# Gated attention and channel MLP on one core: both heads' maxima fetched by one transfer, first stacks loaded two units sooner, two PSUM pairs renamed in turn

## The chip, the cores and the metric

The kernel runs on one core of one Trainium2 chip. A time is the device time of one execution in microseconds (us); the profile is one execution recorded by the hardware, and its span runs from the first to the last recorded instruction. Engines are called as the profile calls them: PE (matmuls), DVE, ACT, POOL, and SP, which here only issues transfers. ACT issues some transfers too.

## The reference

```python
def _A_ref(x, wqkv, wo):
    B, S, D = x.shape
    H = 32; Dh = D // H; W = 256
    qkv = (lambda x, *d: x.transpose(*d))((x @ wqkv).reshape(B, S, 3, H, Dh), 2, 0, 3, 1, 4)
    q, k, v = qkv[0], qkv[1], qkv[2]
    scores = jnp.einsum("bhqd,bhkd->bhqk", q, k) * (Dh ** -0.5)
    idx = jnp.arange(S)
    mask = (idx[:, None] - idx[None, :] >= 0) & (idx[:, None] - idx[None, :] < W)
    scores = jnp.where(mask[None, None], scores, -1e9)
    p = _softmax(scores, axis=-1)
    o = jnp.einsum("bhqk,bhkd->bhqd", p, v)
    return (lambda x, *d: x.transpose(*d))(o, 0, 2, 1, 3).reshape(B, S, D) @ wo
...
def _B_ref(x, w1, b1, w2, b2):
    y = _layernorm(x, axis=-1)
    h = _gelu(jnp.einsum("bsd,df->bsf", y, w1) + b1)
    return jnp.einsum("bsf,fd->bsd", h, w2) + b2
...
g = _sigmoid((x * gate_w).sum(-1, keepdims=True))
a = _A_ref(x, A_wqkv, A_wo)
b = _B_ref(x, B_w1, B_b1, B_w2, B_b2)
return g * a + (1 - g) * b
```

There are 2048 tokens (S) of 512 numbers, 32 heads of 16 numbers with a window of 256 tokens, and a hidden width of 1792. All is float32.

## The kernel before

Products are made in several passes: a number is split into a high part, rounded to a shorter format, and a low part, the remainder, and high x high, low x high and high x low are added up. The work has three stages.

**First stage: projections.** A list of `units` is run one by one. A unit is one product of 12 matmuls of 512 columns: `qk_unit(g, t, c)` for a group g of 8 heads, q or k (t), and a chunk c of 512 tokens, or `v_unit(b)` for 128 tokens. `plan` says what is done before which unit: `at(n, fn)` puts fn before unit n, and what was put first under one n is done first. `after(k, fn)` postpones fn by k units. The result of a `qk_unit` is split and written to a DRAM tensor `qkd[g, t]`, which holds for each of the 8 heads a stack of rows: high, low and high again for k (high, high, low for q), 48 rows in all, and 2 gap rows. `gaps(g)` fills the gap rows from rows of the SBUF tensor `qk` that were set to a constant. `load_stacks(p, a, n)` brings for the four heads of step p (two pairs `pr` of heads, of two heads `e` each) n columns from column a back into `qk`, 14 partitions down, so that the two heads of a pair lie above each other. The result goes to `qs` (q) and `ks` (k), which are halves of `qk`. Besides, weights (`load_w`, the line L228), rows of x for the layer norm's sums (`stat_unit`, L468), and constants (`load_consts`) are loaded. From unit 16 on the first scores are made as well.

**Second stage: attention, mixed with the MLP's first half.** A string `ORDER` lists the steps: S is `s_pair`, the scores of 128 queries for two heads, of which only the row maximum is wanted; T is `st_pair`, the scores again, transposed, from which the maximum is subtracted within the matmul (that takes two more rows: high and low part of the maximum on the side of q, -1 on the side of k), with the exponential and the mask after it; P is `pv`, the product with v; f is one matmul pair of the MLP. After four blocks of queries `put_max` carries their maxima to the rows of `qs`: `parts` splits them on POOL, `turn` transposes them on DVE, `put` writes them to a DRAM tensor `md` (from ACT's queue in this stage), and `rest` loads them from `md` (SP's queue). They come 6, 13, 21 and 28 steps later (`CHAIN`). An S, T or f step takes its two PSUM banks from `ring`: `choose()` takes out a name at a place that `PICK` gives, and the name goes back at the end.

**Third stage:** the second half of the MLP, the output projection and the gate.

SP carries its transfers out in the order of the program, and each is issued when what it needs has come; a wait holds up all transfers behind it. The program gives every transfer one of 8 semaphores in turn, so that at most 8 of both queues are under way.

Of the kernel before, what the change touches and what calls it, by code (L numbers as in the profile page):

```python
# [13 lines left out]
F32R = mybir.dt.float32r  # L14
# [8 lines left out]
DH = 16  # L23
# [8 lines left out]
HG = H // NG  # L32
VW = 17
VR = 560
EPS = 1e-5
NEG = -3.0e38
U8 = mybir.dt.uint8
# [24 lines left out]
def gated_mix_kernel(ctx, tc: tile.TileContext, xt, x2, wq0, wqk, wv, wo, xa, gw, w1, w2, b1, b2, out):  # L62
# [96 lines left out]
    osc = dram.tile([8, 128, S], F32, name="osc")  # L159
    stat = dram.tile([2, 2, S // 2], F32, name="stat")  # L160
    hp = dram.tile([NCH, FT, 128, C], F32, name="hp")
    qkd = {(g, t): dram.tile([HG, 50, S], F32R, name=f"qk{g}_{t}") for g in range(NG) for t in range(2)}

    open_pool("w")
    open_pool("ring")
# [52 lines left out]

    def gaps(g):
        for t in range(2):  # L220
            sp.dma_start(f32(view(qkd[g, t], [50 * S, HG], [S, 2], [1, S], off=48 * S)), f32(ks[0][112:128]))

    wq, wvs, xh, xl = {}, [], [], []

# [87 lines left out]
    def qk_out(g, t, c, o):  # L312
        d = qkd[g, t]
        h, l = t2(F32R), t2(F32R)
        copy(h, o)
        lo_part(l, o, h)

        def put(eng, k, s):
            eng.dma_start(f32(view(d, [S, DH], [50 * S, HG], [1, C], off=k * DH * S + c * C)), f32(s))

        if g:
            put(act, 0, h)
        late = (2, 1, 1, 1)[c] if not g else 1
        after(late, lambda: [put(sp, k, h) for k in ((0, 1 + t) if not g else ())])
        after(late, lambda: put(sp, 2 - t, l))

    def double(g, c, t):
        fr, to = (f32(view(qkd[g, t], [S, DH], [50 * S, HG], [1, C], off=k * DH * S + c * C)) for k in (0, 1 + t))
        sp.dma_start(to, fr)

    def v_unit(b):
# [12 lines left out]
    def load_stacks(p, a, n):  # L344
        g, j = divmod(p, 2)
        held_cols[p] = a + n
        for t in (1, 0):
            src = view(qkd[g, t], [S, 98], [100 * S, 2], [1, n], off=4 * j * 50 * S + a)
            sp.dma_start(f32(qk[14:112, 2 * t:2 * t + 2, a:a + n]), f32(src))

    mxs, done = {}, set()

    def s_pair(p, qb, pr):
        if qb == 0 and pr == 0:
            mxs[p] = small("mx", 2, (128, 2, 2, NB))
        assert qb * 128 < held_cols[p]
        n = min(qb + 1, 3) * 128
        t0 = qb * 128 + 128 - n
        o = two()
        for e in range(2):  # L360
            r, k = ((0, 62), (64, 112))[e]
            pe.matmul(o[:, e, :n], qs[pr][r:k, qb * 128:qb * 128 + 128], ks[pr][r:k, t0:t0 + n],  # L362
                      start=True, stop=True)
        m = mxs[p][:, pr, :, qb]
        if qb < 2:
            for e in range(2):
                sc = small("scr", 2, (128, 256), BF16)
                dve.tensor_tensor_reduce(out=sc[:, :n], in0=o[:, e, :n], in1=wide[:, 256 - n:], scale=1.0, scalar=NEG,
                                         op0=ALU.add, op1=ALU.max, accum_out=m[:, e:e + 1])
        else:  # L370
            dve.copy_predicated(o[:, :, :128], tri, o[:, :, 256:384])  # L371
            dve.tensor_reduce(m, o[:, :, :256], mybir.AxisListType.X, ALU.max)  # L372
        if pr and qb % 4 == 3:
            put_max(p, qb - 3)

    def put_max(p, a):
        mx = mxs[p][:, :, :, a:a + 4]
        sm = {}
        md = dram.tile([2, 2, 2, 4, 128], F32R, name=nm("md"))

        def parts():
            m = sm["m"] = small("nm", 2, (128, 2, 2, 2, 4), F32R)
            pool.tensor_copy(m[:, 0], mx)
            lo_part(m[:, 1], mx, m[:, 0], pool)

        def turn():
            sm["s"] = small("ms", 2, (128, 32))
            dve.transpose(sm["s"], f32(sm["m"]).rearrange("p a b c d -> p (a b c d)"))

        def put(eng=None):  # L390
            (eng or (act if spot[0] > 99 else sp)).dma_start(f32(view(md, [32, 4], [128, 32], [1, 32])), sm["s"])

        def rest():
            done.add(("m", p, a // 4))
            for k in range(2):
                src = view(md, [512, 2], [1024, 2], [1, 512], off=2048 * k)
                sp.dma_start(f32(qk[62 + k:113 + k:50, :2, a * 128:a * 128 + 512]), f32(src))
# [574 lines left out]
```

## Time and profile before

| | |
|---|---|
| runs | 691.52, 687.71, 690.15 us; median 690.15 |
| profiled execution | 688.9 us, of which the span takes 686.9 |
| mean granted PE clock | 0.999 |
| busy share of the span | PE 99%, DVE 69%, ACT 56%, POOL 39% |
| transfers | 137.91 MB, mean 201 GB/s |

The first stage lasts until 144 us, the second until 486 us. In a timeline row the first number is the start in us from the span's start, the second the length, then engine (SPq: the issue of a transfer), line, operation, what is written from what, the shapes, the count of merged instructions, and in brackets the engine's idle time before it with what ended that. A row of waits has the total in us, the number of times, and the longest. A row of the chain has start, length and what it was.

### The profile page before, as it was taken

The page shows a single profiled execution, that of the slowest core. Times are in us where ns is not written, and L with a number is a line of the kernel's source. Part 1 is how long each engine was busy: PE and PEld are TensorE (multiplying, and loading weights), DVE is VectorE, ACT ScalarE, POOL GpSimd, SP SyncE. Part 2 cuts the span into 40 slices and gives each one's busy share as a digit, 9 for nine tenths or more (in the row PEclk, how much of TensorE's full clock was granted, in tenths as well). Part 3 has the DMA queues.
Part 4 walks back from the last instruction along what each step waited for, and adds up shares of the span by engine and source line. Part 5 has one row for each costly group of instructions (what it writes and reads, how often), then busy time and mean ns, then how long its engine had stood idle before and what let it go on. Part 6 is the DMA issues. An engine that isn't in the chain of part 4 may idle for free.

```text
span 686.9 us, 15594 instructions
## 1 busy us (share of the span) xinstructions
PE 680.0 (99%) x5674; PEld 532.7 (78%) x5674; DVE 473.3 (69%) x970; ACT 387.4 (56%) x637; POOL 266.6 (39%) x622
## 2 busy tenths in 40 slices
PE   9999999999999999999999999999999999999997
PEld 6887777877767877778787777777787888888886
DVE  6737789958767788787777777856575545556454
ACT  6437554456777776767667777677633224123221
POOL 5800166335566664756655666568000000000000
PEclk9999999999999999999999999999999999999999
DMA  8999898776755867656775655436886440841701
GB/s 314 361 314 280 263 272 254 223 234 201 227 169 180 249 207 228 190 166 220 222 233 189 177 184 164 159 127 211 291 235 209 140 171 5 270 132 45 251 0 62
DMA packets 89620, 137.91 MB, mean 201 GB/s; under 512 B 13160, under 2 KB 36648, under 8 KB 89416
## 3 DMA queue, kind: packets, MB, share of 16 engines
q1 hardware_dynamic: 81384, 128.72, 59.3%
q10 hardware_dynamic: 8160, 8.19, 3.8%
q8 instruction: 45, 0.74, 0.5%
q14 instruction: 31, 0.25, 0.1%
HBM read 81.53 MB, written 54.30 MB: 198 GB/s over the span
## 4 chain that ended last, share of the span: by engine, by line
PE 90%; DMA 6%; DVE 1%; SPq 1%; issue 0%; ACT 0%; DVEq 0%; ACTq 0%
PE ps_b L651 22%; PE ps_a L881 16%; PE ps_b L441 12%; PE ps_d L308 12%; PE ps_b L418 7%; PE ps_d L338 7%; PE ps_b L362 6%; PE ps_o L850 6%; DMA oa<-osc 1%; DMA md<-ms 1%; DMA ra<-rd 1%; DMA su<-osc 1%; PE ps_d L295 1%; PE ps_x L362 1%; DMA hp<-t 1%; PE ps_x L279 1%
## 5 line engine op out<-in xcount | busy, mean ns | idle before, releaser
L651 PE MATMUL ps_b<-x,w 64*128 64x512 f32 x1344 | 208.1, 393 | 0.1
L881 PE MATMUL ps_a<-x,t 128*128 128x512 f32 x648 | 150.7, 390 | 0.2 <-DVE t L711 0.2
L372 DVE TENSOR_REDUCE mx<-ps_b 128x2 f32<-128x512 f32 x208 | 144.2, 693 | 7.2
L881 PEld LDWEIGHTS ps_a<-x,t 128*128 128x128 f32 x648 | 121.3, 188 | 26.8 <-DVE t L133 0.8
L651 PEld LDWEIGHTS ps_b<-x,w 64*128 64x128 f32 x1344 | 125.9, 186 | 11.1 <-issue 0.6
L371 DVE COPY_PREDICATED ps_b<-tri,ps_b 128x256 f32<-128x256 uint8 x208 | 88.4, 425 | 53.9 <-PE ps_b L362 39.9
L422 POOL TENSOR_SCALAR_AFFINE_SELECT pa<-pa 128x256 f32<-128x256 f32 x192 | 74.2, 413 | 63.8 <-ACT pa L420 63.3
L420 ACT ACTIVATE pa<-ps_b 128x768 f32<-128x768 f32 x96 | 76.8, 812 | 25.5 <-PE ps_b L418 17.0
L418 PE MATMUL ps_b<-qk 64*128 64x384 f32 (+4 forms) x512 | 87.6, 339 | 1.2 <-DMA qk<-md 1.1
L308 PE MATMUL ps_d<-x,w 128*128 128x512 f32 x360 | 84.7, 390 | 0.0
L362 PE MATMUL ps_b<-qk 62*128 62x384 f32 (+3 forms) x472 | 82.3, 344 | 0.0
L308 PEld LDWEIGHTS ps_d<-x,w 128*128 128x128 f32 x360 | 67.3, 188 | 14.5 <-issue 0.5
L420 ACT ACTIVATE pb<-ps_b 128x768 f32<-128x768 f32 (+2 forms) x96 | 66.5, 706 | 18.2 <-PE ps_b L418 14.7
L422 POOL TENSOR_SCALAR_AFFINE_SELECT pb<-pb 128x256 f32<-128x256 f32 x160 | 62.5, 414 | 31.4 <-ACT pb L420 29.7
L707 ACT ACTIVATE t<-t,b1s 128x512 f32<-128x512 f32 x56 | 38.5, 716 | 45.6 <-DMA t<-hp 45.0
L422 POOL TENSOR_SCALAR_AFFINE_SELECT x<-x 128x256 f32<-128x256 f32 x128 | 49.4, 413 | 36.0 <-ACT x L420 35.3
L418 PEld LDWEIGHTS ps_b<-qk 50*128 50x128 f32 (+1 forms) x512 | 48.6, 184 | 17.8 <-DVE mx L372 2.5
L420 ACT ACTIVATE x<-ps_b 128x768 f32<-128x768 f32 x64 | 51.0, 812 | 15.8 <-PE ps_b L418 9.4
L362 PEld LDWEIGHTS ps_b<-qk 62*128 62x128 f32 (+1 forms) x472 | 44.8, 184 | 16.7 <-issue 4.5
L338 PE MATMUL ps_d<-wv,x 128*128 128x512 f32 x192 | 46.7, 394 | 0.0
L850 PE MATMUL ps_o<-w,t 128*128 128x512 f32 x192 | 46.1, 389 | 0.0
L441 PE MATMUL ps_b<-pa,v 128*32 128x128 f32 (+2 forms) x704 | 42.9, 345 | 0.2
(96 smaller groups left out, 753.7 us busy)
## 6 DMA issues: line engine op xcount, KB each, us to landing
qk<-qk SPq DMA_DIRECT2D x112, 196.0 KB
t<-hp SPq DMA_DIRECT2D x56, 256.0 KB
hp<-t SPq DMA_DIRECT2D x54, 256.0 KB
qk<-t SPq DMA_DIRECT2D x48, 256.0 KB
osc<-x SPq DMA_DIRECT2D x31, 256.0 KB
t<-in_w SPq DMA_DIRECT2D x28, 256.0 KB
w<-w SPq DMA_DIRECT2D x28, 256.0 KB
qk<-t ACTq DMA_DIRECT2D x24, 256.0 KB
```

The lines of the kernel that those rows point to most:

```text
L308: pe.matmul(o, a[:, dt * 128:(dt + 1) * 128], b[:, dt * C:(dt + 1) * C], start=n == 0, stop=n == 11)
L338: pe.matmul(o, x[:, a:a + 128], wvs[dt][:, k], start=n == 0, stop=n == 11)
L362: pe.matmul(o[:, e, :n], qs[pr][r:k, qb * 128:qb * 128 + 128], ks[pr][r:k, t0:t0 + n], start=True, stop=True)
L371: dve.copy_predicated(o[:, :, :128], tri, o[:, :, 256:384])
L372: dve.tensor_reduce(m, o[:, :, :256], mybir.AxisListType.X, ALU.max)
L418: pe.matmul(o[:, e, :w], ks[pr][r:k, kb * 128:kb * 128 + 128], qs[pr][r:k, kb * 128:kb * 128 + w], start=True, stop=True)
L420: act.activation(pt[:, :, :w], o[:, :, :w], AF.Exp, scale=0.25)
L422: pool.affine_select(out=pt[:, :, a:a + 128], in_=pt[:, :, a:a + 128], pattern=[[0, 2], [sgn, 128]], base=b, channel_multiplier=-sgn, comp ...
L441: pe.matmul(a[32 * h:32 * h + 32, at:at + w], vs[:, kb, v:v + 32], pts[p, kb][:, h, fr:fr + w], start=n == 0, stop=n == len(parts) - 1, sk ...
L651: pe.matmul(o[:, e], w[kt // 4][r:r + 64, k, m:m + 128], y[r:r + 64, a:a + C], start=n == 0, stop=n == 23)
L850: pe.matmul(a, x[:, g], wos[g][:, k], start=n == 0, stop=n == 11)
L881: pe.matmul(accs[c][b], x[:, b * 128:(b + 1) * 128], w, start=f == 0 and n == 0, stop=f == FT - 1 and n == 2)
```

## The change

It has four parts.

1. *One transfer for the maxima.* The stacks in `qkd` get 52 rows per head instead of 50, so that the gap between the two heads of a pair is four rows, and the second head begins on partition 66. `md` and the tile `nm` are laid out by head first, and `rest` loads four neighbouring partitions (62 to 65) by one transfer where it loaded two partitions by each of two. `load_stacks` brings 100 partitions (14 to 113), where it brought 98. The second head's scores in `s_pair` run over 50 partitions, where they ran over 48.
2. *Gap rows.* They are four rows, of which `gaps` now fills only those between the heads of a pair, for q from rows set to 0 and for k from rows set to -1. Each transfer has 8 pieces of 16 KB where it had 16 of 8 KB.
3. *Places in the plan.* `gaps(0)` stands before unit 7 (was 8), the first `load_stacks` before unit 9 (was 11), and both stand ahead of `load_consts` in the code.
4. *Ring.* It starts as b0, b1, b3, b2.

```diff
+HR = 52
...
-    qkd = {(g, t): dram.tile([HG, 50, S], F32R, name=f"qk{g}_{t}") for g in range(NG) for t in range(2)}
+    qkd = {(g, t): dram.tile([HG, HR, S], F32R, name=f"qk{g}_{t}") for g in range(NG) for t in range(2)}
...
     def gaps(g):
         for t in range(2):
-            sp.dma_start(f32(view(qkd[g, t], [50 * S, HG], [S, 2], [1, S], off=48 * S)), f32(ks[0][112:128]))
+            dst = view(qkd[g, t], [2 * HR * S, 4], [2 * S, 2], [1, 2 * S], off=48 * S)
+            sp.dma_start(f32(dst), f32(qk[116 * t:116 * t + 8, 2:].rearrange("k r s -> k (r s)")))
...
-            src = view(qkd[g, t], [S, 98], [100 * S, 2], [1, n], off=4 * j * 50 * S + a)
-            sp.dma_start(f32(qk[14:112, 2 * t:2 * t + 2, a:a + n]), f32(src))
+            src = view(qkd[g, t], [S, 100], [2 * HR * S, 2], [1, n], off=4 * j * HR * S + a)
+            sp.dma_start(f32(qk[14:114, 2 * t:2 * t + 2, a:a + n]), f32(src))
...
-            r, k = ((0, 62), (64, 112))[e]
+            r, k = ((0, 62), (64, 114))[e]
...
-        md = dram.tile([2, 2, 2, 4, 128], F32R, name=nm("md"))
+        md = dram.tile([4, 2, 4, 128], F32R, name=nm("md"))
...
-            pool.tensor_copy(m[:, 0], mx)
-            lo_part(m[:, 1], mx, m[:, 0], pool)
+            mt = mx.rearrange("p r e b -> p e r b")
+            pool.tensor_copy(m[:, :, 0], mt)
+            lo_part(m[:, :, 1], mt, m[:, :, 0], pool)
...
-            for k in range(2):
-                src = view(md, [512, 2], [1024, 2], [1, 512], off=2048 * k)
-                sp.dma_start(f32(qk[62 + k:113 + k:50, :2, a * 128:a * 128 + 512]), f32(src))
+            sp.dma_start(f32(qk[62:66, :2, a * 128:a * 128 + 512]), f32(view(md, [1024, 4], [512, 2], [1, 512])))
...
+    for g in range(NG):
+        at((7, 16, 20, 24)[g], lambda g=g: gaps(g))
+    for c in range(NCH):
+        at((9, 19, 29, 44)[c], lambda c=c: load_stacks(0, c * C, C))
     at(9, load_consts)
-    for g in range(NG):
-        at((8, 16, 20, 24)[g], lambda g=g: gaps(g))
-    for c in range(NCH):
-        at((11, 19, 29, 44)[c], lambda c=c: load_stacks(0, c * C, C))
...
-    ring += ["b0", "b1", "b2", "b3"]
+    ring += ["b0", "b1", "b3", "b2"]
```

From here the order of the built programs. The line numbers of the changed kernel are one or two higher. The numbers in a name tell one buffer or tensor from another. First SP's queue in the first stage, around units 9 to 12 (t: an SBUF tile; qk0_0 and qk0_1: the stacks in DRAM for q and k of group 0; qk_3_79: the SBUF tensor `qk`), before:

```order
L319 DMA qk0_0_65<-t_63_415 16x8x512
L463 DMA gws_9_99<-in_gw 128x512
L464 DMA b1s_83<-in_b1 128x14
L468 DMA t_64_423<-in_xa 128x512
L228 DMA t_66_426<-in_wqk 128x512
L319 DMA qk0_1_66<-t_68_441 16x8x512 x2
L319 DMA qk0_1_66<-t_69_442 16x8x512
L468 DMA t_70_448<-in_xa 128x512
L349 DMA qk_3_79<-qk0_1_66 98x2x512
L349 DMA qk_3_79<-qk0_0_65 98x2x512
L468 DMA t_72_468<-in_xa 128x512
L228 DMA t_74_471<-in_wqk 128x512
```

And the same rows of SP's queue in the changed kernel:

```order
L321 DMA qk0_0_65<-t_63_415 16x8x512
L351 DMA qk_3_79<-qk0_1_66 100x2x512
L351 DMA qk_3_79<-qk0_0_65 100x2x512
L464 DMA gws_9_99<-in_gw 128x512
L465 DMA b1s_83<-in_b1 128x14
L469 DMA t_64_425<-in_xa 128x512
L230 DMA t_66_428<-in_wqk 128x512
L321 DMA qk0_1_66<-t_68_443 16x8x512 x2
L321 DMA qk0_1_66<-t_69_444 16x8x512
L469 DMA t_70_450<-in_xa 128x512
L469 DMA t_72_468<-in_xa 128x512
L230 DMA t_74_471<-in_wqk 128x512
```

The two stack loads (L349, now L351) have moved ahead of eight transfers: the two constants, two loads of x rows, one weight load, and the three writes that stand between the latter. From the last load of x rows shown on, all stands as before. The gap transfers of group 0 (L221, now L223) stand four rows ahead of these pieces, in the same place before and now, since the order in the code makes up for the earlier unit; only their shape is another, 4x2x4096 where it was 8x2x2048.

In the second stage, SP's queue around the sixth load of maxima, before and then in the changed kernel:

```order
L349 DMA qk_3_79<-qk0_1_66 98x2x256
L349 DMA qk_3_79<-qk0_0_65 98x2x256
L397 DMA qk_3_79<-md_288_2053 2x2x512 x2
L541 DMA t_295_2239<-in_w1 128x512
L349 DMA qk_3_79<-qk1_1_68 98x2x256
```

```order
L351 DMA qk_3_79<-qk0_1_66 100x2x256
L351 DMA qk_3_79<-qk0_0_65 100x2x256
L398 DMA qk_3_79<-md_288_2048 4x2x512
L542 DMA t_295_2233<-in_w1 128x512
L351 DMA qk_3_79<-qk1_1_68 100x2x256
```

Nothing moved there but the second of the two loads of maxima, which is gone; so it is at all 32 places.

Last PE at the first steps of the attention, before and then in the changed kernel (ps_b0 to ps_b3 are the PSUM pairs of the ring):

```order
L362 MATMUL ps_b0_260_1529<-qk_3_79 128x384 x2
L418 MATMUL ps_b1_261_1535<-qk_3_79 128x384 x2
L651 MATMUL ps_b2_262_1541<-x8_142_850,w_218_1285 128x512 x2
L362 MATMUL ps_b3_263_1544<-qk_3_79 128x384 x2
L651 MATMUL ps_b2_262_1541<-x8_142_850,w_218_1285 128x512 x6
```

```order
L364 MATMUL ps_b0_260_1527<-qk_3_79 128x384 x2
L419 MATMUL ps_b1_261_1533<-qk_3_79 128x384 x2
L652 MATMUL ps_b3_262_1539<-x8_142_850,w_218_1283 128x512 x2
L364 MATMUL ps_b2_263_1542<-qk_3_79 128x384 x2
L652 MATMUL ps_b3_262_1539<-x8_142_850,w_218_1283 128x512 x6
```

The matmuls stand as before; the names b2 and b3 are exchanged, here and in all later rows. A pool hands out its banks in the order in which its names are first used: in the built program the third pair (b2 before, b3 now) is banks 4 and 5, and the fourth is banks 6 and 7, before and now.

More of the change, by code (lines that the diff above doesn't have):

```diff
@@ L318, in put @@
         def put(eng, k, s):
-            eng.dma_start(f32(view(d, [S, DH], [50 * S, HG], [1, C], off=k * DH * S + c * C)), f32(s))
+            eng.dma_start(f32(view(d, [S, DH], [HR * S, HG], [1, C], off=k * DH * S + c * C)), f32(s))
         if g:
@@ L327, in double @@
     def double(g, c, t):
-        fr, to = (f32(view(qkd[g, t], [S, DH], [50 * S, HG], [1, C], off=k * DH * S + c * C)) for k in (0, 1 + t))
+        fr, to = (f32(view(qkd[g, t], [S, DH], [HR * S, HG], [1, C], off=k * DH * S + c * C)) for k in (0, 1 + t))
         sp.dma_start(to, fr)
```

## The prediction

> **What bounds the kernel now.** I read the page's first part, then PE's waits, then the chain and the timelines around those waits.
>
> ```profile
> span 686.9 us, 15594 instructions
> PE 680.0 (99%) x5674; PEld 532.7 (78%) x5674; DVE 473.3 (69%) x970; ACT 387.4 (56%) x637; POOL 266.6 (39%) x622
> ```
>
> PE works 680.0 of 686.9 us, so an edit that leaves PE's instructions as they are can gain at most the 6.9 us of idle time. This one leaves them: same matmuls, same columns, same order; only the second head's scores are summed over 50 partitions for 48. Which waits are in the 6.9 us?
>
> ```profile
> PE ps_x L279 <- DVE t L275: 1.3, 1, 1.3
> PE ps_b L418 <- DMA qk<-md: 1.1, 2, 0.9
> PE ps_a L881 <- DVE t L711: 0.2, 1, 0.2
> ```
>
> These are all of PE's waits inside the span, 2.6 us (total, times, longest). The rest stands at the ends, where nothing is changed. Only the middle row touches the change: twice `st_pair` waits for maxima. PE's timeline shows where:
>
> ```profile
> 192.62 0.61 PE L418 MATMUL ps_b<-qk 64*128 64x384 f32 x4 [0.90 <-DMA qk<-md]
> ...
> 255.95 0.44 PE L418 MATMUL ps_b<-qk 64*128 64x384 f32 x2 [0.19 <-DMA qk<-md]
> ```
>
> **One transfer for the maxima.** The chain of waits shows what lies ahead of the two matmuls (start, length, what):
>
> ```profile
> 184.85 4.73 DMA md<-ms
> ...
> 189.65 0.66 SPq L397
> ...
> 190.36 2.13 DMA qk<-md
> 192.49 0.14 issue
> 192.62 0.61 PE ps_b L418 x4
> ```
>
> ```profile
> 249.12 3.92 DMA md<-ms
> ...
> 253.06 0.66 SPq L397
> ...
> 253.76 2.06 DMA qk<-md
> 255.82 0.14 issue
> 255.95 0.44 PE ps_b L418 x2
> ```
>
> The write to `md` lands, SP issues the first load (0.66 us), then the second, and the chain runs through the second: it sets out at 190.36, which is 189.65 plus 0.66 plus a pause of 0.05. SP's timeline shows the pair merged:
>
> ```profile
> 189.65 1.34 SPq L397 DMA_DIRECT2D qk<-md  x2
> ```
>
> With one transfer this second issue falls away, so the maxima land earlier by 190.36 - 189.65 = 0.71 us at the first place and by 253.76 - 253.06 = 0.70 at the second. What is unknown is how long a transfer of four partitions and 16 KB takes to land. The bounds: as long as the 8 KB ones (2.06 and 2.13), or as long as the other 16 KB transfer, `md<-ms` (3.92 and 4.73), which writes memory where this one reads it. With the first the gain is 0.71 of 0.90 and all of the 0.19, **0.90 us**; with the second the load lands 1.1 to 1.9 us later than now, which costs that much at each of the two places, 3.0 us, and opens waits at others. I take the first: it is the same direction, the same piece of 2 KB and the same two tensors.
>
> The other 30 loads have no wait on PE today. They too come 0.7 us earlier, and gain nothing. SP is spared 32 issues of 0.66, 21 us; what does it do with them?
>
> ```profile
> SPq L397 <- DMA md<-ms: 66.5, 28, 4.4
> ```
>
> It waits for the maxima's writes anyway, 66.5 us in 28 places (4.4 the longest), and the transfers queued behind a load of maxima are issued 0.7 us sooner. PE waits for none of them (its three rows of waits name no other transfer), so nothing: 0. What limits the gain: after the first place PE arrives at each later matmul 0.71 us sooner, while writes that were already under way do not. Between 0 and 0.90 us can come back as a new wait; I take 0, since the maxima follow from PE's own scores and move with them.
>
> POOL's two operations on `nm` write their 16 columns in another order: two instructions before and after. Their cover is the 13 to 28 steps between the first of `CHAIN` and the last; the count of elements is the same, so 0; at the two waiting places whatever they take more would show in full.
>
> **The stacks' shape.** Each stack load has 100 rows for 98, 2% more bytes. In the second stage the transfers have room:
>
> ```profile
> 140.00:480.00 340.00, 338.50 (x4140) 258.79 (x4140) 256.89 (x578) 248.76 (x380) 209.14 (x551) 1.00 0.64 197
> ```
>
> (The columns: window, sum, busy PE, PEld, DVE, ACT, POOL, granted PE clock, DMA share, GB/s.) At a share of 0.64, 2% are nothing: 0. How far 100 rows instead of 98 spread over the DMA engines, no row shows; that is part of the rival below.
>
> **Gaps and first stacks, sooner.** Here the transfers are the tight resource:
>
> ```profile
> 10.00:30.00 20.00, 20.00 (x90) 16.57 (x89) 18.14 (x25) 11.10 (x20) 18.68 (x17) 1.00 1.05 390
> 30.00:43.00 13.00, 13.00 (x59) 10.78 (x58) 4.92 (x8) 3.52 (x6) 3.02 (x2) 1.00 0.91 293
> 43.00:56.00 13.00, 13.00 (x62) 10.27 (x61) 6.85 (x22) 8.09 (x21) 0.00 (x0) 1.00 0.97 324
> ```
>
> The DMA share is 0.91 to 1.05, yet PE is busy throughout. SP's timeline:
>
> ```profile
> 29.04 1.67 SPq L221 DMA_DIRECT2D qk<-qk  x2
> ...
> 34.20 0.60 SPq L463 DMA_DIRECT2D gws<-in_gw  x1
> ...
> 36.55 0.43 SPq L228 DMA_DIRECT2D t<-in_wqk  x1
> 37.08 1.80 SPq L319 DMA_DIRECT2D qk<-t  x3
> 38.92 0.86 SPq L468 DMA_DIRECT2D t<-in_xa  x1
> 39.88 1.33 SPq L349 DMA_DIRECT2D qk<-qk  x2
> 41.32 0.42 SPq L468 DMA_DIRECT2D t<-in_xa  x1
> 41.78 0.43 SPq L228 DMA_DIRECT2D t<-in_wqk  x1
> ```
>
> In the new order the two stack loads (39.88) go out at 34.20, and the eight transfers from `gws` to the `in_xa` of 38.92 follow 1.33 us later. The gap transfers (29.04) keep their place, and the last of their source rows have been set by 19.9:
>
> ```profile
> 16.09 3.84 POOL L207 MEMSET qk<- 32x2048 f32 x2
> ```
>
> Nothing gains by earlier stacks: their first user has no wait. Who loses? The weight load that was ahead of the stacks and is now behind them:
>
> ```profile
> 41.01 0.43 DVE L194 CAST w<-t 128x512 fp32r<-128x512 f32 x1 [4.56 <-DMA t<-in_wqk]
> 41.47 0.69 DVE L133 TENSOR_TENSOR w<-t,w 128x512 fp32r<-128x512 f32 x1
> 42.29 0.69 DVE L133 TENSOR_TENSOR t<-ps_d,t 128x512 fp32r<-128x512 f32 x1
> ...
> 50.05 0.43 DVE L194 CAST w<-t 128x512 fp32r<-128x512 f32 x1 [2.89 <-PE ps_x L362]
> ...
> 54.88 0.08 DVE L368 DVE_READ_ACCUMULATOR2_ANT mx<- 128x1 f32 x1
> ```
>
> It is issued at 36.55 and cast at 41.01, the moment it lands: 4.46 us. The next, of equal size but behind the stack pair, is issued at 41.78 and cast at 50.05: 8.27 us. So a stack pair costs the transfer behind it up to 8.27 - 4.46 = 3.81 us. The first weight load then is issued near 37.9 and lands between 42.3 (its issue + 4.46) and 46.1 (+ 8.27). What it feeds on PE begins here:
>
> ```profile
> 49.71 0.44 PE L362 MATMUL ps_x<-qk 62*128 62x128 f32 x4
> 50.08 3.00 PE L308 MATMUL ps_d<-x,w 128*128 128x512 f32 x12
> ...
> 55.73 0.50 PE L362 MATMUL ps_x<-qk 62*128 62x256 f32 x4
> ```
>
> The product at 50.08 uses the weights that DVE casts from 41.01 on, and the PSUM bank that DVE's 42.29 row reads, which is queued behind the cast. With the cast at 46.1, cast (0.43), remainder (0.69) and that row (0.69) end by 48.0, 2.1 us before PE gets there: hidden. The load behind, of 41.78, no longer has the pair before it and comes sooner or, the path being full all the way, at the same time: 0, since the same bytes go ahead of it as before.
>
> **The ring** exchanges two names. The order of the banks follows from first use, so PE's matmuls stand on the same banks with the same distances: 0, in both directions.
>
> **Sum.** 688.9 of the profiled execution (its span of 686.9 and 2.0 around it) - 0.71 - 0.19 + 0 = 688.0. That execution lies 1.25 below the median of the three runs (690.15), and all four (687.71, 688.9, 690.15, 691.52) spread by 3.8; I take their middle, (688.9 + 690.15) / 2 = 689.5, and forecast 689.5 - 0.9 = **688.6 us**. A change of less than 0.5%, 3.45 us (686.7 to 693.6), can hardly be told from none in a measurement of this kernel.
>
> **Rival 1: the gain doesn't come.** The single transfer of four partitions and 16 KB lands 0.7 us later than two 8 KB ones did, or the next late write takes the wait over. For it: the writes to `md` take 3.92 to 4.73 us in the chain, the largest share, and they aren't touched. Against: SP's second issue is plainly serial. The time: 689.5.
>
> **Rival 2, slower: the new shapes hold the full DMA path longer, and PE stalls in the first stage.** A gap transfer now has four slowest rows (was eight), a stack load 100 (was 98). No row shows what that does to the landing. If fewer DMA engines carry a transfer, those behind it wait. The place is the weight load that DVE casts at 50.05. From there DVE works without a pause to 54.96 (54.88 + 0.08), the last maximum of the scores at 49.71, and the second scores on PE at 55.73 need their PSUM banks back: a margin of 55.73 - 54.96 = 0.77 us. That is the point that decides: if the load comes more than about 0.8 us later, the rest is a stall of PE. Gaps with half the rows, taken to last twice as long, make the load later by their share of the pair's price: two of 128 KB against two of 392 KB, 3.81 x 256 / 784 = 1.24 us. A stack pair that lasts 1.5 times as long, halfway between nothing and double, adds 1.90. By the gaps alone PE stalls 1.24 - 0.77 = 0.5, by both 1.24 + 1.90 - 0.77 = 2.4, by a doubled pair alone 3.81 - 0.77 = 3.0; with the gain of 0.9 that is 689.1, 691.0 and 691.6. Beyond a delay of 0.77 + 0.90 = 1.7 us the kernel is slower than before. I take 691.0. For it: shares of 0.91 to 1.05, and DVE's waits for weights in the rows. Against it: stack loads of 98 rows run in all of the kernel now without making PE wait.
>
> The Trainium skill has a rule on this, on its page "DMA: Bandwidth & Descriptors", section "Why a DMA increments its semaphore by 16 and not by 1": a transfer uses the largest number of engines up to 16 that divides the slowest dimension of both sides, and the page's own example is 100 partitions on 10 engines. By that rule 98 rows go on 14 engines and 100 on 10 (the factor 1.4), gap transfers go from 8 engines to 4 (the factor two), and the loads of maxima from 2 to 4; as an estimate from that page and the pair's 3.81 us, the load at 50.05 comes 0.4 x 3.81 + 1.24 = 2.8 us later and the time is 688.6 + 2.8 - 0.8 = 690.6. No row here shows the engines of one transfer, so the rule is neither borne out nor refuted yet.
>
> **How the numbers follow.** Gain of 0.9 with the first stage hidden: 0.46, at 688.6. Rival 1: 0.17, at 689.5. Rival 2: 0.33, at 691.0. Something not seen here: 0.04. The low end is the fastest run less the gain, 687.71 - 0.9 - 0.2 for the chance of a bit more = 686.6; the high end is rival 2's 691.6 plus 0.7 for the spread of medians = 692.3. All three cases lie inside 0.5%. Faster by more needs the gain and a fast draw: 0.07. Slower by more needs rival 2 beyond its own top or a slow draw: 0.08. That leaves 0.85.
>
> **What the profile of the changed kernel would show.** Right: PE's row of waits for `qk<-md` falls from 1.1 to about 0.2 us, the first place's wait from 0.90 to 0.2, the chain there holds one SP issue, and the chain's `qk<-md` piece is still about 2.1 us. Wrong by rival 1: that piece is 2.8 us or more, or a wait of like size stands at another load of maxima. Wrong by rival 2: PE's timeline has an idle piece ahead of the scores near 55.7 us, released by DVE, and DVE's casts there wait for `in_wqk` past 51 us; in the second stage PE would wait for `qk<-qk`. The forecast falls if PE's busy time itself moves from 680.0 us.

## The result

The changed kernel is slower: 699.29 us median of 6 runs (694.54 to 702.39), the kernel before 690.84 of 6 (687.71 to 692.72); ratio 1.0133, 95% interval 1.0103 to 1.0164. The forecast was 688.6 us, range 686.6 to 692.3. Of all executions in this document one, of 709.70 us in the run b_md4 below, lies more than 1.5% above the fastest of its kernel; it counts as slow and is left out.

The profiled execution took 702.17 us, one of the two slowest of the six, so its losses are larger than the median's. The page:

```profile
span 700.4 us, 15571 instructions
PE 685.5 (98%) x5674; PEld 538.5 (77%) x5674; DVE 473.8 (68%) x970; ACT 385.4 (55%) x637; POOL 267.8 (38%) x622
```

The span grew by 13.5 us: PE is busy 5.5 us longer with the same 5674 matmuls, and idle 8.0 us longer (14.9 for 6.9). PE's waits (total, times, longest) say where the idle time is:

```profile
PE ps_x L364 <- DVE mx L374: 4.3, 3, 3.6
PE ps_x L364 <- DVE mx L370: 2.4, 1, 2.4
PE ps_b L419 <- DMA qk<-md: 2.3, 2, 2.1
PE ps_x L281 <- DVE t L277: 1.3, 1, 1.3
PE ps_a L882 <- DVE t L712: 0.2, 1, 0.2
```

Two rows are new: the first scores (`ps_x`, L364 was L362) wait 6.7 us for DVE. The row of the maxima has not fallen from 1.1, it has grown to 2.3. The same on PE's timeline:

```profile
58.72 0.83 PE L364 MATMUL ps_x<-qk 62*128 62x256 f32 x4 [2.41 <-DVE mx L370]
...
106.07 0.69 PE L364 MATMUL ps_x<-qk 62*128 62x384 f32 x2 [3.64 <-DVE mx L374]
...
202.64 0.62 PE L419 MATMUL ps_b<-qk 64*128 64x384 f32 x4 [0.28 <-DMA qk<-md]
...
247.83 0.44 PE L419 MATMUL ps_b<-qk 64*128 64x384 f32 x2 [2.05 <-DMA qk<-md]
```

The first is the place of rival 2. What leads to it is on the timelines of SP, ACT and DVE. SP's first, and the row of the one wait it has at these loads:

```profile
37.60 0.75 SPq L351 DMA_DIRECT2D qk<-qk  x2
...
39.99 0.65 SPq L230 DMA_DIRECT2D t<-in_wqk  x1
```

```profile
SPq L351 <- DMA qk<-qk: 1.1, 1, 1.1
```

The stacks go out at 37.60, where the prediction had 34.20: SP waits 1.1 us for the gap transfers, and the issues ahead take longer too. The weight load now behind the stacks is issued at 39.99 and cast at 48.77 (DVE's first row below), where it was issued at 36.55 and cast at 41.01. A write of a projection's result, issued at 40.73 behind them, lands at 49.49 (its last completion event), 8.76 us later. ACT issues such writes too, and its next one has the same one of the eight semaphores: it waits for that landing, and ACT's work behind it waits with it. ACT's row after this wait, before and then in the changed kernel, and a later one there:

```profile
43.77 0.63 ACT L471 ACTIVATE waste<-t 128x512 f32<-128x512 f32 x1 [1.51 <-DMA qk<-t]
```

```profile
50.24 0.63 ACT L472 ACTIVATE waste<-t 128x512 f32<-128x512 f32 x1 [7.69 <-DMA qk<-t]
...
56.33 0.58 ACT L137 ACTIVATE t<-ps_d 128x512 fp32r<-128x512 f32 x1
```

So ACT goes on 6.5 us later than before. From 50.24 to the end of the last of these rows it works, or issues, without a pause, and DVE waits for it twice:

```profile
48.77 0.43 DVE L195 CAST w<-t 128x512 fp32r<-128x512 f32 x1 [9.42 <-DMA t<-in_wqk]
...
52.33 0.69 DVE L134 TENSOR_TENSOR t<-ps_d,t 128x512 fp32r<-128x512 f32 x1 [1.80 <-ACT t L137]
...
53.54 0.42 DVE L195 CAST w<-t 128x512 fp32r<-128x512 f32 x1
...
56.94 0.69 DVE L134 TENSOR_TENSOR t<-ps_d,t 128x512 fp32r<-128x512 f32 x1 [0.58 <-ACT t L137]
...
59.02 0.08 DVE L370 DVE_READ_ACCUMULATOR2_ANT mx<- 128x1 f32 x1
```

So the maxima of the first scores end by 59.1 instead of 54.96, and PE goes on at 58.72, with the first of their banks.

Third, PE's busy time. The windows around the second stall (sum; busy PE, PEld, DVE, ACT, POOL; granted PE clock, DMA share, GB/s), and those around 247.8:

```profile
100.00:105.00 5.00, 2.43 (x11) 1.67 (x9) 4.93 (x11) 3.00 (x8) 2.07 (x3) 1.00 0.77 225
105.00:110.00 5.00, 3.55 (x9) 2.45 (x10) 4.53 (x9) 1.73 (x4) 4.09 (x14) 0.59 0.78 216
110.00:115.00 5.00, 5.00 (x18) 3.96 (x17) 4.23 (x8) 1.12 (x2) 2.33 (x4) 0.73 0.95 320
...
245.00:260.00 15.00, 12.95 (x128) 11.14 (x122) 8.58 (x18) 8.09 (x12) 5.76 (x16) 0.89 0.64 210
```

After these two stalls the granted clock is 0.59, 0.73 and 0.89, where the kernel before ran at 0.999 in the mean. At most 5 x 0.41 + 5 x 0.27 + 15 x 0.11 = 5.1 us of PE's 5.5 us of additional busy time are that.

For what follows I cut each execution at PE's first matmul into `ps_b` (start of the attention) and its first into `ps_a` (its end). Before, then changed:

```profile
144.27 0.44 PE L362 MATMUL ps_b<-qk 62*128 62x384 f32 x2
...
485.60 0.73 PE L881 MATMUL ps_a<-x,x 128*128 128x512 f32 x2
```

```profile
155.33 0.44 PE L364 MATMUL ps_b<-qk 62*128 62x384 f32 x2
...
499.47 0.73 PE L882 MATMUL ps_a<-x,x 128*128 128x512 f32 x2
```

First stage 144.3 to 155.3, attention 341.3 to 344.1, third stage 201.3 to 200.9: in this execution the first stage has most of the loss.

The trace also has each transfer's issue and its completion events. A landing in the text is the last of these, and their number is not the same for all: a stack load of 98 rows has 15 events, one of 100 rows 11; a gap transfer 9 before and 5 now. The Trainium skill, page "DMA: Bandwidth & Descriptors", section "Why a DMA increments its semaphore by 16 and not by 1", lets one event come at once and one from each DMA engine taking part; then 98 rows are on 14 engines, 100 on 10, and gaps on 4 where they were on 8, as the rule of the largest divisor says. The trace agrees with it here, and below for 102 and 104 rows.

### The profile page after: what moved, and what is told of

It is laid out like the page before. It is cut to its first block, busy times and chain, and to the rows that moved or that the text cites. A ratio compares the mean times of both kernels' runs of the same rounds, so it can differ in the third digit from the quotient of the medians.

```text
span 700.4 us, 15571 instructions
## 1 busy us (share of the span) xinstructions
PE 685.5 (98%) x5674; PEld 538.5 (77%) x5674; DVE 473.8 (68%) x970; ACT 385.4 (55%) x637; POOL 267.8 (38%) x622
## 4 chain that ended last, share of the span: by engine, by line
PE 75%; DMA 16%; DVE 4%; ACT 2%; SPq 1%; issue 1%; ACTq 0%; POOL 0%; DVEq 0%
PE ps_b L652 22%; PE ps_a L882 16%; PE ps_b L442 12%; PE ps_b L419 7%; PE ps_b L364 6%; PE ps_o L851 6%; DMA t<-in_xa 4%; PE ps_d L310 4%; PE ps_d L340 3%; DMA qk<-qk 2%; DMA md<-ms 2%; DMA ra<-rd 1%; DMA t<-in_x 1%; DMA oa<-osc 1%; DMA su<-osc 1%
## 5 line engine op out<-in xcount | busy, mean ns | idle before, releaser
L652 PEld LDWEIGHTS ps_b<-x,w 64*128 64x128 f32 x1344 | 128.2, 187 | 10.1 <-issue 0.6
L419 PE MATMUL ps_b<-qk 50*128 50x384 f32 (+5 forms) x512 | 88.5, 339 | 2.3 <-DMA qk<-md 2.3
L364 PE MATMUL ps_b<-qk 62*128 62x384 f32 (+3 forms) x472 | 83.6, 347 | 0.0
L364 PEld LDWEIGHTS ps_b<-qk 62*128 62x128 f32 (+1 forms) x472 | 45.4, 186 | 17.1 <-issue 4.5
L340 PE MATMUL ps_d<-wv,x 128*128 128x512 f32 x192 | 48.9, 408 | 0.0
L851 PE MATMUL ps_o<-w,t 128*128 128x512 f32 x192 | 46.1, 389 | 0.0
L340 PEld LDWEIGHTS ps_d<-wv,x 128*128 128x128 f32 x192 | 37.2, 196 | 9.3 <-issue 1.5
```

What stands on the lines that cost most here:

```text
L340: pe.matmul(o, x[:, a:a + 128], wvs[dt][:, k], start=n == 0, stop=n == 11)
L419: pe.matmul(o[:, e, :w], ks[pr][r:k, kb * 128:kb * 128 + 128], qs[pr][r:k, kb * 128:kb * 128 + w], start=True, stop=True)
L652: pe.matmul(o[:, e], w[kt // 4][r:r + 64, k, m:m + 128], y[r:r + 64, a:a + C], start=n == 0, stop=n == 23)
L851: pe.matmul(a, x[:, g], wos[g][:, k], start=n == 0, stop=n == 11)
```

## Experiments

Theories: **spread** (the rows of a transfer divide over fewer DMA engines, so it holds them longer), **place** (the stacks' earlier place delays the weights), **maxima** (the single transfer), **bytes** (more rows, more bytes on a full path). Times are medians; the kernel before, beside them, ran at 689.3 to 689.9. The stages are those of one execution each.

| run | us | ratio (95%) | first stage, attention (us, profiled execution) |
|---|---|---|---|
| b_gap4 (= before again) | 689.07 | 0.9997 (0.9977 to 1.0016) | 144.7, 339.8 |
| b_stack100 | 698.20 | 1.0124 (1.0094 to 1.0155) | 145.6, 349.9 |
| b_rows104 | 696.30 | 1.0096 (1.0072 to 1.0120) | 152.3, 339.8 |
| b_gapsrc | 695.37 | 1.0083 (1.0058 to 1.0108) | 151.1, 341.5 |
| b_rows102 | 726.74 | 1.0534 (1.0483 to 1.0585) | 158.7, 367.2 |
| b_gap2 | 699.46 | 1.0143 (1.0106 to 1.0181) | 155.2, 341.5 |
| b_md4 | 699.28 | 1.0145 (1.0124 to 1.0166) | 144.5, 350.7 |
| b_stack104 | 707.91 | 1.0262 (1.0245 to 1.0280) | 165.3, 339.7 |
| fixgap | 693.52 | 1.0058 (1.0039 to 1.0078) | 147.8, 344.2 |
| place_back | 701.57 | 1.0160 (1.0111 to 1.0208) | 149.0, 342.5 |
| fixboth | 710.42 | 1.0318 (1.0287 to 1.0349) | 167.3, 339.9 |
| fixlate | 699.44 | 1.0141 (1.0124 to 1.0159) | 149.0, 346.3 |
| fixlate_place | 701.63 | 1.0169 (1.0141 to 1.0197) | 149.5, 348.5 |
| cand | 699.30 | 1.0149 (1.0106 to 1.0192) | 155.4, 342.3 |

**The stacks' rows alone, in the kernel before (b_stack100).**

```diff
-            src = view(qkd[g, t], [S, 98], [100 * S, 2], [1, n], off=4 * j * 50 * S + a)
-            sp.dma_start(f32(qk[14:112, 2 * t:2 * t + 2, a:a + n]), f32(src))
+            src = view(qkd[g, t], [S, 100], [100 * S, 2], [1, n], off=4 * j * 50 * S + a)
+            sp.dma_start(f32(qk[14:114, 2 * t:2 * t + 2, a:a + n]), f32(src))
```

> The kernel before with one edit: each stack load brings 100 rows to 100 partitions, where it brought 98 (the two rows more are gap rows and land where nothing reads them); gaps, maxima, places as before. Theory 'shape' (100 rows are spread over fewer DMA engines than 98, each load holds the path longer, DVE gets its weights and x rows late and PE stalls at the first scores): most of the loss is here, 694 to 700 us, with PE waits on DVE at ps_x of 3 us or more in the first stage. Theory 'place' (the stacks' earlier place delays the weights): no change, 689 to 692. Theory 'maxima' (the single transfer is at fault): no change as well.

698.2 us: two more rows cost as much as the whole change. But the loss is not where I expected it: the first stage grew by 1.3 us, the attention by 8.6. Its waits on PE:

```profile
PE ps_b L418 <- DMA qk<-md: 3.1, 1, 3.1
PE ps_b L441 <- ACT pa L420: 1.5, 1, 1.5
...
PE ps_b L362 <- DMA qk<-qk: 1.1, 1, 1.1
```

From issue to landing a stack load of the attention takes 4.33 us (median), for 3.47 before. 'Place' and 'maxima' can't explain this run.

**The gaps' pieces, a first try (b_gap4).** The target was written as `[100 * S, 4], [50 * S, 2], [S, 2], [1, S]`; the first two steps can be joined, and the built program is that of before.

> The kernel before with one edit: the gap transfers' target is given as four pieces of 2x2 rows, where it was eight of 2; bytes, places, stacks and maxima as before. Theory 'shape': gap transfers take up to twice as long, a smaller loss than the stacks', 690.5 to 694 us, with a PE wait of 0.3 to 2 us near the first scores. Theories 'place' and 'maxima': no change, 689 to 692.

So this is a second sample of before. It shows one thing: its profiled execution has no wait for maxima at all, and its attention takes 339.8 us, 1.5 less than in the first profile:

```profile
PE ps_x L279 <- DVE t L275: 1.3, 1, 1.3
PE ps_a L881 <- DVE t L711: 0.2, 1, 0.2
```

The 1.1 us that the change was to remove are not there in every execution.

**Rows as a dose (b_rows104, b_rows102).** 104 rows are more bytes than 100 but divide better; 102 are between, and divide worse. Even steps p only: the rows beyond 100 are read from the next pair of the group, and at an odd step the second pair has none behind it. The diff is that of 104; the other run has 102 in its place.

```diff
-            src = view(qkd[g, t], [S, 98], [100 * S, 2], [1, n], off=4 * j * 50 * S + a)
-            sp.dma_start(f32(qk[14:112, 2 * t:2 * t + 2, a:a + n]), f32(src))
+            m = 98 if j else 104
+            src = view(qkd[g, t], [S, m], [100 * S, 2], [1, n], off=4 * j * 50 * S + a)
+            sp.dma_start(f32(qk[14:14 + m, 2 * t:2 * t + 2, a:a + n]), f32(src))
...
-            sp.dma_start(f32(view(qkd[g, t], [50 * S, HG], [S, 2], [1, S], off=48 * S)), f32(ks[0][112:128]))
+            sp.dma_start(f32(view(qkd[g, t], [50 * S, HG], [S, 2], [1, S], off=48 * S)), f32(qk[120:128, 2:].rearrange("k r s -> k (r s)")) if g else f32(ks[0][112:128]))
```

> The kernel before with stack loads of 104 rows at even steps p (the first stage's loads among them), 98 at odd steps as before; no transfer is added. The gap transfers of groups 1 to 3 take the same constants from eight other partitions. Theory 'spread' (104 divides over 13 engines, 98 over 14): near before, 688.5 to 693 us, and the attention 340 to 342 us long. Theory 'bytes' (6% more): worse than 100 rows, above 698.

> As the run before it, with 102 rows where it has 104: fewer bytes, but by the theory 'spread' 6 DMA engines instead of 13. Theory 'spread': much slower than the 698.2 of 100 rows at all steps, 705 to 740 us, the longest waits on stacks and on DVE in both stages. Theory 'bytes': between before and its neighbour, 688 to 700.

In the attention the order is 104 and 98 rows (339.8 us; 341.3, and 339.8 in the second sample), 100 (349.9), 102 (367.2, though half its loads keep 98 rows). Completion events are 14, 15, 11 and 7, so 13, 14, 10 and 6 engines; median landings of the loads with these rows in the attention are 3.36, 3.47, 4.33 and 6.14 us. Bytes order them otherwise (98, 100, 102, 104). This settles the stacks: spread. PE's largest waits in the run with 102 rows are for stacks, and for maxima whose transfers share the path:

```profile
PE ps_b L419 <- DMA qk<-md: 8.6, 5, 3.0
PE ps_b L363 <- DMA qk<-qk: 6.3, 7, 1.9
PE ps_x L363 <- DVE mx L373: 4.3, 4, 2.8
PE ps_x L363 <- DMA qk<-qk: 4.0, 2, 2.1
```

104 rows were not free in the first stage, though (152.3 us), against my expectation for the whole.

**The gaps' source alone (b_gapsrc).** The last two lines of the diff above, with 98 rows.

> The kernel before with one edit: the gap transfers of groups 1 to 3 take the same constants from eight partitions of 16 KB, where they took sixteen of 8 KB; stack loads keep 98 rows. Theory 'spread, and the gaps' source is what slowed the first stage of the 104-row run' (152.3 us for 144.3): 692 to 697 us, the first stage 148 us or longer. Theory 'the 6% more bytes of the 104 rows slowed it': 688.5 to 691, the first stage 144 to 146.

695.4 us and a first stage of 151.1: the source explains what 104 rows left open. The six gap transfers of groups 1 to 3 keep 8 pieces and 9 events, and only read 8 partitions of 16 KB for 16 of 8 KB; their median landing is 7.60 us, where it was 5.89 (5.43 in the second sample of before). One stall of the first scores carries most of it:

```profile
102.22 0.69 PE L362 MATMUL ps_x<-qk 62*128 62x384 f32 x2 [3.18 <-DVE mx L372]
```

The change reads its gap rows from 8 partitions of 16 KB as well. Why that is slower on as many engines no run shows.

**The gaps' pieces (b_gap2, fixgap).** In the kernel before, two pieces for eight; in the changed one, eight for four.

```diff
-            sp.dma_start(f32(view(qkd[g, t], [50 * S, HG], [S, 2], [1, S], off=48 * S)), f32(ks[0][112:128]))
+            sp.dma_start(f32(view(qkd[g, t], [S, 2], [50 * S, HG], [1, S], off=48 * S)), f32(ks[0][112:128]))
```

> The kernel before with the gap transfers' target in another order: two pieces of 8 rows where it had eight of 2; the same bytes, places, and number of transfers (an earlier run that asked for four pieces of 2 x 2 rows turned out to build the very program of before, since the steps can be joined; its 0.9997 is thus a second sample of before). Theory 'spread': each gap transfer takes some 4 times as long, the transfers behind it are late and the first stage grows by 4 to 20 us: 694 to 710. Theory 'only the stacks count': 688.5 to 692.

```diff
-            dst = view(qkd[g, t], [2 * HR * S, 4], [2 * S, 2], [1, 2 * S], off=48 * S)
+            dst = view(qkd[g, t], [4 * S // 8, 8], [2 * HR * S, 4], [1, 4 * S // 8], off=48 * S)
```

> The changed kernel with the gap transfers alone cut otherwise: eight pieces of 4 x 1024 columns, where it had four of 2 x 4096, the same bytes; stack loads stay at 100 rows. Theory 'the stacks' rows are the loss': still slow, 695 to 701 us. Theory 'the gaps' four pieces are the loss in the first stage': 689 to 694, with the first stage (144.3 us before, 155.3 changed) back below 147.

Eight transfers with two pieces (3 events, landing 8.39 us for 5.19) cost the kernel before 10.1 us, all of it in the first stage. Giving the changed kernel its eight pieces back took its first stage from 155.3 to 147.8 us and its ratio from 1.0133 to 1.0058. So I was wrong to expect that the stacks' rows alone would keep it at 695 or above: both shapes are at fault, and in the changed kernel the four pieces, in the first stage, cost the larger part. The attention stayed at 344.2 with the wait at the same place:

```profile
PE ps_b L419 <- DMA qk<-md: 2.3, 2, 2.0
PE ps_x L364 <- DVE mx L370: 1.6, 1, 1.6
```

**The places (place_back).** The changed kernel with the three plan entries of before.

```diff
-    for g in range(NG):
-        at((7, 16, 20, 24)[g], lambda g=g: gaps(g))
-    for c in range(NCH):
-        at((9, 19, 29, 44)[c], lambda c=c: load_stacks(0, c * C, C))
     at(9, load_consts)
+    for g in range(NG):
+        at((8, 16, 20, 24)[g], lambda g=g: gaps(g))
+    for c in range(NCH):
+        at((11, 19, 29, 44)[c], lambda c=c: load_stacks(0, c * C, C))
```

> The changed kernel with the gaps back at unit 8, the first stacks back at unit 11 and the constants ahead of both; shapes, maxima and ring as changed. Theory 'shape': still slow, 694 to 700 us, stalls at later first scores as in the changed kernel. Theory 'place': 688.5 to 691. Theory 'maxima': 696 to 700.

701.6 us, not distinguishable from 699.3 (the profiled execution, 695.37, is by 6 us the fastest of its four, so its stages show less than the median has). Taking the earlier place back gains nothing. It moves a stall: the one of 2.41 us at 58.72 is not there, and with the slow shapes the later place makes PE wait, at 51.5, for the stacks themselves, which it did not at unit 9:

```profile
PE ps_x L364 <- DMA qk<-qk: 1.9, 1, 1.9
```

**Two issues more (b_md4).** The kernel before with four transfers of one partition for each set of maxima.

```diff
-                src = view(md, [512, 2], [1024, 2], [1, 512], off=2048 * k)
-                sp.dma_start(f32(qk[62 + k:113 + k:50, :2, a * 128:a * 128 + 512]), f32(src))
+                for e in range(2):
+                    src = view(md, [1024, 2], [1, 512], off=2048 * k + 512 * e)
+                    sp.dma_start(f32(qk[62 + k + 50 * e:63 + k + 50 * e, :2, a * 128:a * 128 + 512]), f32(src))
```

> The kernel before with the maxima brought by four transfers of one partition each, where it had two of two partitions: the suspected cost, an issue of 0.66 to 0.70 us, is added twice more. Theory 'the last issue is on the path at one or two places' : PE's waits for maxima grow from 1.1 to about 4 us in all, 691.5 to 695 us. Theory 'these waits come and go from run to run and the issue is mostly hidden': within 1 us of before, 689 to 691.

699.3 us, above both expectations; the attention grew by 9.3 us. Waits for stacks and for maxima came up at nine places:

```profile
PE ps_b L362 <- DMA qk<-qk: 3.0, 3, 1.3
PE ps_b L419 <- DMA qk<-md: 3.0, 6, 1.1
```

64 more transfers on SP delay what stands behind them, so a transfer saved there can be worth time. Whether it is their issues that cost it, or the semaphores of the eight that they take up in turn, this run doesn't separate, and the waits are only part of the 9.3 us: PE's busy time grew too, to 683.8 us, at a granted clock of 1.00. In the other direction there is little left to win, as the next runs show.

**Better shapes at the changed layout (b_stack104, fixboth, fixlate, fixlate_place, cand).** With 52 rows per head a load of 104 rows includes trailing gap rows, which must be filled by transfers of their own; b_stack104 has the like in the kernel before, four rows per stack and the gap source of b_gapsrc, for all groups. The loads are edited alike, here fixboth; the gaps have eight pieces:

```diff
-            src = view(qkd[g, t], [S, 100], [2 * HR * S, 2], [1, n], off=4 * j * HR * S + a)
-            sp.dma_start(f32(qk[14:114, 2 * t:2 * t + 2, a:a + n]), f32(src))
+            src = view(qkd[g, t], [S, 104], [2 * HR * S, 2], [1, n], off=4 * j * HR * S + a)
+            sp.dma_start(f32(qk[14:118, 2 * t:2 * t + 2, a:a + n]), f32(src))
...
+            dst = view(qkd[g, t], [4 * S // 8, 8], [2 * HR * S, 4], [1, 4 * S // 8], off=48 * S)
+            src = f32(qk[120 * t:120 * t + 8, 2:].rearrange("k r s -> k (r s)"))
+            sp.dma_start(f32(dst), src)
+            sp.dma_start(f32(view(qkd[g, t], [4 * S // 8, 8], [2 * HR * S, 4], [1, 4 * S // 8], off=(HR + 48) * S)), src)
```

> The kernel before with stack loads of 104 rows (partitions 14 to 117; the six rows more are gap rows and rows of the next pair, which nothing reads there), where it had 98; for that each stack in DRAM gets four rows more at its end, filled by one 32 KB transfer each (8 in all, in the first stage), and the gap transfers take their constants from eight partitions. Rows of 100 gave 698.2 us. Theory 'spread' (what counts is over how many DMA engines the rows divide: 98 over 14, 104 over 13, 100 over 10): about the time of before, 688.5 to 692.5 us, 6% more bytes included. Theory 'bytes' (more rows, more bytes, a path that is full): worse than 100 rows, 698 to 710.

> The changed kernel with other shapes alone: stack loads of 104 rows (14 to 117, with the trailing gap rows, which are now filled by a second pair of gap transfers per group, so 256 KB more per group), and gap transfers of eight pieces. Places, the single transfer for the maxima and the ring as changed. Theory 'shape': the stalls of the first stage and the 8.4 us write of maxima near 237 us go, 688 to 691 us, PE waiting for maxima 0.3 us or less. Theory 'place': 696 to 700 with the stalls still there. Theory 'maxima': 696 to 700, with the waits for maxima still above 2 us.

> The changed kernel with stack loads of 104 rows and gap transfers of eight pieces as in the run before with both, but with the first stage relieved: for group 0 the trailing rows are filled for two pairs only before the first stacks (128 KB, the rest at unit 34), and the gaps of groups 1 to 3 go to units 36, 39 and 42 (they stood at 16, 20 and 24). Theory 'spread' with the added gap bytes as the cause of the 710.4: first stage 144 to 147 us, attention 339.9, 687 to 691 us in all. Theory 'the earlier place of the stacks hurts by itself': 693 to 700, with stalls at ps_x near 50 to 60 us.

> As the run before it, with the first stacks back at unit 11 and the first gaps back at unit 8, behind the constants. Theory 'spread': the places matter by less than 2 us either way, 687 to 691 us. Theory 'the earlier place hurts': faster than its neighbour by 3 us or more.

> The changed kernel made as good as its layout allows: stack loads of 104 rows, gap transfers of eight pieces at the changed places, and the trailing rows filled by transfers of their own, for the first two pairs at unit 6, for the rest at units 26 to 34, where the transfers have more room than at 34 to 42 in the run that waited 4.0 us at the attention's start. Theory 'spread, with any added transfer in the first stage costing time': attention 339.7 to 340.5 us, first stage 146 to 156, 690 to 702 in all, not better than before. Theory 'the change's idea is sound once its shapes are right': first stage below 146, 686.5 to 690.

The attention of fixboth takes 339.9 us without one wait on PE, and b_stack104's 339.7: with 13 engines the changed attention is as fast as the best of the kernel before, with one transfer for the maxima (fixboth) or with two (b_stack104, b_rows104: 339.8). So there the single transfer gains nothing beyond what before reaches in some executions; cand, with the same attention, still waited 1.6 us for maxima. The first stage lost much more than I had expected in both, 167.3 and 165.3 us. That b_stack104's 707.9 us lie where theory 'bytes' had them comes from this stage, not from the loads of the attention. The added fills and the source of 8 partitions both fall into it; what each costs there wasn't separated. fixboth:

```profile
PE ps_x L366 <- DVE mx L376: 10.5, 6, 4.0
```

fixlate and cand fill less ahead of the first stacks and put the rest later. `gaps(g, 1, j, n)` fills the trailing rows of n pairs from pair j on; the first piece is fixlate's, the second cand's, which keeps the other gaps at units 7, 16, 20 and 24:

```diff
+    at(7, lambda: (gaps(0), gaps(0, 1, 0, 2)))
+    at(34, lambda: gaps(0, 1, 2, 2))
+    for g in range(1, NG):
+        at((0, 36, 39, 42)[g], lambda g=g: (gaps(g), gaps(g, 1)))
...
+    at(6, lambda: gaps(0, 1, 0, 2))
+    for g in range(NG):
+        at((26, 28, 31, 34)[g], lambda g=g: gaps(g, 1, 0 if g else 2, 4 if g else 2))
```

That moved the stalls, to 4.0 us on the stacks early in the attention (158.9) in fixlate and to the scores at 123.5 (3.1 us) in cand, and both stand at 699 us. fixlate_place puts fixlate's stacks back at unit 11 and its first gaps at unit 8: 701.6, so again nothing is gained by it. None of these beats the kernel before.

## Why the prediction was wrong

**What was right.** The first waiting place went as worked out: the chain has one issue less, and the transfer of four partitions takes 2.17 us, close to the lower bound that I took. From the start of the maxima's write to the landing of the load it is 7.03 us (202.50 - 195.47) for 7.64 before (192.49 - 184.85), with a write that took 0.11 longer, and the wait fell from 0.90 to 0.28 us (0.2 forecast):

```profile
195.47 4.84 DMA md<-ms
200.31 0.02 issue
200.33 2.17 DMA qk<-md
202.50 0.14 issue
202.64 0.62 PE ps_b L419 x4
```

The second place, with its 0.19, has no wait now. But b_gap4, which is the kernel before with its two loads, waits at neither: at the first its write landed after 3.53 us for 4.73. The 0.9 us were a matter of that one execution, and no run measures this gain in the time of the whole kernel.

The moved places (0): taking them back gained nothing in two pairs of runs (place_back, fixlate_place), but it moved a stall. The ring (0) and the single transfer were not tried by themselves, nor the earlier places with the shapes of before.

**Step that failed: "At a share of 0.64, 2% are nothing: 0".** I sized the stack load by its bytes and by the mean share of the path, and set aside how its rows divide. b_stack100 puts that term at +8.4 us (698.20 - 689.85), most of it in the attention, where I had seen room: the mean over 16 engines hides that ten of them carry a whole load. In the changed kernel it more than undoes the gain, at a load of maxima that had no wait before: the write of these maxima, issued behind three stack loads of the same 2 us, lands after 8.41 us where it took 5.45 before, the longest of that stage, and PE waits 2.05 us there. The same write took 8.91 us in b_stack100 and 8.01 in fixgap, both with 100 rows, and 2.99 in fixboth with 104.

```profile
237.01 8.41 DMA md<-ms
245.42 0.02 issue
245.43 0.02 SPq L398
245.45 0.04 issue
245.49 2.21 DMA qk<-md
```

**Step that failed: "hidden", in the first stage.** I looked for the loser among the weight loads alone, and let the moved one land by 46.1 at the latest, from a pair price of 3.81 us that holds for the old shapes. It was cast at 48.77, since the pair went out late, behind gap transfers that land more slowly, and was slower itself. Even so PE's product of these weights began at 50.58 without a wait of note. What I left out is ACT: its own next transfer waited behind the same pair, ACT stood still for 7.69 us instead of 1.51, and DVE, and by it PE, waited for ACT. The gaps' four pieces carry much of the loss: with eight (fixgap) the first stage is 7.5 us shorter, this stall is 1.6 us for 2.41, and the later one of 3.64 us is 0.6.

Rival 2 had the place right. That its stall with both shapes slower, 2.4 us, is near the profile's 2.41 is in part luck. It counted on the weight load that was cast at 50.05 to come 3.1 us later; this load landed 2.6 us later (52.58, where it was 49.96), and was cast at 53.54 without a wait for `in_wqk`, against the sign given, because DVE was still at work that had waited for ACT. And its margin of 0.77 us ran to the last maximum, while PE went on 0.38 us before that was done (59.10 - 58.72). Above all its price was that of one place in one stage. A larger stall came later in the first stage (3.64 us at 106.07) and one in the attention, so 691.0, and with it the range's top of 692.3, was too low by some 8 us. The page's rule that stood beside it holds; its estimate of 690.6 failed for the same reason, one place instead of all that these shapes pass through.

**Left out: the clock.** I held PE's 680.0 us of busy time fixed. Two of the three long stalls were followed by some microseconds of lower clock, at most 5.1 us in the profiled execution.

**The shapes don't add up.** Stack rows alone +8.4 us, the gaps' source alone +6.0 (695.37 - 689.34), and the whole change, with four pieces besides, +8.5. fixgap, with both the rows and the source, is at +3.6. It has the single transfer and the earlier places, and b_stack100 has not; whether one of these takes back the difference wasn't isolated. Of the 5.7 us between the attentions of their two profiled executions (349.9 and 344.2), 3.4 are clock: two stalls of b_stack100 were each followed by 0.66 over 5 us, and none of fixgap's was followed by less than 1.00.

## What to carry to other kernels

Before changing a transfer's row count or its outer dimension, work out over how many DMA engines it divides: in the attention 98 and 104 rows were fast, 100 slow and 102 very slow, against their bytes. A mean DMA share well below 1 is no cover for such a transfer. For a transfer that is moved ahead, ask not only which load comes later, but whose own transfers wait behind it, as ACT's did here. And a delay found at one place should be priced at every place the shape passes through, with the clock that can be lost after a stall.

## What the runs showed of the hardware

**The clock after a stall.** In the run b_stack100 a stall of 1.49 us at 154.7 was enough:

```profile
154.00:157.00 3.00, 1.51 (x24) 0.74 (x20) 2.23 (x5) 2.30 (x4) 1.61 (x3) 1.00 0.66 235
157.00:162.00 5.00, 5.00 (x34) 4.09 (x34) 2.67 (x6) 2.79 (x4) 2.12 (x7) 0.66 0.34 100
```

0.66 over 5 us is 1.7 us lost, more than the stall itself. The length alone does not decide: the stall of 2.41 us in the changed kernel, one of 2.0 in fixgap and one of 2.6 in b_rows102 were followed by 1.00, the changed kernel's of 2.05 by 0.66. Those of 2.9 to 3.6 us were followed by 0.50 to 0.66 over the next 5 us (the changed kernel's second, b_stack100's at 239, b_gap2, b_rows104, cand). The Trainium skill, page "TensorE: Matmul & The Clock Gate", section "Part 1: The HAM clock gate (the "warmup" mystery)", has the clock halved after an idle window of about 3.4 us that runs freely; the size of the loss agrees (3.4 us at half speed is 1.7 lost), but here a stall of less than half that length was enough.

**Source partitions.** A gap transfer of 128 KB with eight pieces on its target landed after 7.60 us instead of 5.89 (medians of six) when it read 8 partitions of 16 KB for 16 of 8 KB, and these six cost the kernel 6.0 us.
